# Two adjacent tokens per partition, and weights staged in fp32 and cast on chip: a recurrent attention kernel with a feed-forward layer

## The chip, the cores and the metric

The kernel runs on one core of one Trainium2 chip. The metric is the device time of one execution in microseconds (us), lower is better. Three runs of the kernel before gave a median of 203.13 us (202.38 to 204.61).

The engines are named as in the profile: PE is TensorE's matrix multiply, PEld its weight load, DVE VectorE, ACT ScalarE, POOL GpSimd and SP SyncE. A letter q behind an engine's name is its queue of issued transfers.

## The reference, cut to what matters

```python
# q, k, v, alpha: (batch 4, heads 8, sequence 768, head_dim 48), fp32; alpha between 0.8 and 1.0
for t in range(S):
    state = alpha[:, :, t, :, None] * state + einsum('bhd,bhe->bhde', k[:, :, t], v[:, :, t])
    y[:, :, t] = einsum('bhd,bhde->bhe', q[:, :, t], state)
x = y.transpose(0, 2, 1, 3).reshape(3072, 384)
h = x @ w_in                   # 384 x 2048
out = max(h, 0)**2 @ w_out     # 2048 x 384
```

The state decays by alpha at each token. The kernel treats the sequence in chunks of 128 tokens: with the running sum L of log(alpha) inside a chunk, k is scaled by exp(-L) and q by exp(L), and a masked product of both gives the part of y that comes from inside the chunk. There are 24 chunks: 6 for each of 4 batches.

## The kernel before

A small planner inside the program (the class at the top) takes every operation with an assumed duration and a priority, simulates them, and fixes the order of each engine's instructions and the waits between them. On the chip this order does not change any more.

The parts that the change touches, for one chunk g (cuts marked with "..."):

```python
# one transfer per tensor: 128 tokens on 128 partitions, 8 heads of 48 fp32 (pieces of 192 bytes)
for o, (j, t, nm) in enumerate(((3, alpha, "a"), (0, k, "k"), (1, q, "q"), (2, v, "v"))):
    src = t[b, :, t0:t0 + C, :].rearrange("h p d -> p h d")
    dst = RAW[r][:, j, :].rearrange("p (h d) -> p h d", h=H)
    raw_dma[g, nm] = add("sp", lambda e, ...: e.dma_start(dst, src), 650, p0 - 3 * P + o, ...)

# log(alpha), running sum by a matmul with a triangle of ones, exp(-L) and exp(L)
add("act", lambda e: e.activation(lab, RAW[r][:, 3, :]..., AF.Ln), ...)
def m1(pe):
    ins = pe.matmul(psA[:, 0:HD], LTRI[:], lab)
    ...
add("act", lambda e: e.activation(ASB[a][:, 0, :], psA[:, 0:HD], AF.Exp, scale=-1.0), ...)
add("act", lambda e: e.activation(ASB[a][:, 1, :], psA[:, 0:HD], AF.Exp), ...)

# qks: k and q scaled, in one VectorE instruction; then transposed on TensorE (psT), copied (kqt),
# multiplied (psP), masked (pm), and so on
add("dve", lambda e: e.tensor_tensor(QKS[qs][:, :, :, 0:D], RAW[r][:, 0:2, :]..., ASB[a]..., ALU.mult), ...)
...
# the state update takes the scaled k as it lies, a token per partition
ins = pe.matmul(psY[:, p * 96:p * 96 + 96], QKS[qs][:, 0, 2 * p:2 * p + 2, :]..., VBF[vb][:, p * 96:p * 96 + 96])
...
# weights: GpSimd's software queue casts fp32 to bf16 inside the transfer (page of this kernel: 3.15 MB
# in that queue, which is the weights' size in bf16)
wi_dma[i] = add("pool", w_in_dma(i), 800, -1e6 + 3, writes=[("win", i)], ...)
wo_dma[i] = add("pool", w_out_dma(i), 800, -1e4 + i, writes=[("wout", i)], ...)
```

Of the kernel before, what the change touches and what calls it, by code (L numbers as in the profile page):

```python
# [11 lines left out]
class Op:  # L12
# [3 lines left out]
                 "users", "ndeps", "alts")  # L16

    def __init__(self, eng, fn, cost, prio, name):
        self.eng, self.fn, self.cost, self.prio, self.name = eng, fn, cost, prio, name
        self.deps = {}  # L20
        self.lag = 0
        self.sem = None
        self.users = []
        self.pos = None


class Program:
# [14 lines left out]
    def add(self, eng, fn, cost, prio, reads=(), writes=(), name="", dma=None, lag=0, after=()):  # L42
        op = Op(eng, fn, cost, prio, name)
        op.idx = len(self.ops)
        op.lag = lag
        if dma is not None:
            if dma not in self.dma_sems:
                self.dma_sems[dma] = self.nc.alloc_semaphore("d_" + dma)
                self.dma_count[dma] = 0
            self.dma_count[dma] += 1  # L50
            op.sem = (dma, self.dma_count[dma])
# [28 lines left out]
    def schedule(self):  # L80
# [8 lines left out]
        for op in self.ops:  # L89
            op.ndeps = len(op.deps)  # L90
            for d in op.deps:
                d.users.append(op)
            free[op.eng], avail[op.eng], order[op.eng] = 0.0, [], []
            op.start = 0.0
# [20 lines left out]
        def settle(o, at):  # L115
            nonlocal seq
            for u in o.users:
                u.ndeps -= 1
                u.start = max(u.start, at + (self.HOP + (self.TAIL[o.eng] if o.sem is None else 0) if u.deps[o] else 0))
                if u.ndeps == 0:  # L120
                    heapq.heappush(events, (max(u.start, now), seq, "r", u))
                    seq += 1

        while events:
# [40 lines left out]
            for e in avail:  # L165
                while avail[e] and free[e] <= now + 1e-9:
# [6 lines left out]
                    done += 1  # L173
                    if e == "pe":
# [107 lines left out]
def bass_gla_recurrent__then__act_relu_squared_kernel(  # L282
# [12 lines left out]
    assert H == 8 and D == 48 and DM == HD  # L295
# [6 lines left out]
    G = B * NCH  # L302
    chunks = [(b, c) for c in range(NCH) for b in range(B)]

    NRAW, NLAB, NASB, NQKS, NKQT, NPM, NV, NXB, NRR, NGT, NOSB = 6, 2, 3, 3, 3, 2, 4, 2, 4, 7, 3
# [4 lines left out]
    RAW = sb("raw", [128, 4, HD], FP32, NRAW)  # L310
    LAB = sb("lab", [128, H, DP], BF16, NLAB)
    ASB = sb("asb", [128, 2, HD], BF16, NASB)
    QKS = sb("qks", [128, 2, H, DP], BF16, NQKS)
    KQT = sb("kqt", [128, 2, NPR, 128], BF16, NKQT)
    PM = sb("pm", [128, 2, NPR, 128], BF16, NPM)
    VBF = sb("vbf", [128, HD], BF16, NV)
    SBD = sb("sbd", [128, HD], BF16, B)
    TMP = sb("tmp", [128, HD], FP32, 2)
    ACM = sb("acm", [128, 2 * NPR], FP32, 2)
    XBF = sb("xbf", [128, HD], BF16, NXB)  # L320
    XT = nc.alloc_sbuf_tensor("xt", [128, KT, G * C], BF16)
    LTRI = nc.alloc_sbuf_tensor("ltri", [128, 128], BF16)
    IDENT = nc.alloc_sbuf_tensor("ident", [128, 128], BF16)
    ONES2 = nc.alloc_sbuf_tensor("ones2", [128, 2], BF16)
    HSEL = nc.alloc_sbuf_tensor("hsel", [128, 128], BF16)
    HCOL = nc.alloc_sbuf_tensor("hcol", [128, 2 * NPR], BF16)
# [5 lines left out]
    OSB = sb("osb", [128, DM], FP32, NOSB)  # L332

# [19 lines left out]
    def fill(buf, val):  # L353
        return lambda e: e.memset(buf[:], val)  # L354

    def select(buf, op, fill_v, base, pattern, mult):
        return lambda e: e.affine_select(out=buf[:], in_=buf[:], compare_op=op, fill=fill_v, base=base,
                                         pattern=pattern, channel_multiplier=mult)

    warmed = add("dve", fill(WARM, 0.0), 200, -3e6, writes=[("warm",)], name="warm")  # L360
# [10 lines left out]
    for i, t in enumerate(LAB):  # L371
        add("dve", fill(t, 0.0), 300, -1e6, writes=[("lab", i)])
    for i, t in enumerate(QKS):
        add("dve", fill(t, 0.0), 600, -1e6, writes=[("qks", i)])
    add("pool", fill(LTRI, 1.0), 200, -1e6, writes=[("ltri",)])
    add("pool", select(LTRI, ALU.is_ge, 0.0, 0, [[1, 128]], -1), 300, -1e6, reads=[("ltri",)], writes=[("ltri",)])
    add("pool", fill(ONES2, 1.0), 100, -1e6, writes=[("ones",)])

    for buf, key in ((HSEL, "hsel"), (HCOL, "hcol")):
        add("dve", fill(buf, 0.0), 100, -2e6, writes=[(key,)])  # L380
    for part, key, val in ((HSEL[0:1, 64:128], "hsel", -1000.0), (HSEL[32:33, 0:64], "hsel", -1000.0),
                           (HCOL[0:1, 0:2 * NPR:2], "hcol", 1.0), (HCOL[32:33, 1:2 * NPR:2], "hcol", 1.0)):
        add("dve", lambda e, part=part, val=val: e.memset(part, val), 100, -2e6, reads=[(key,)], writes=[(key,)])

    add("pool", fill(IDENT, 0.0), 200, -1e6 + 1, writes=[("ident",)])
    add("pool", select(IDENT, ALU.not_equal, 1.0, 0, [[-1, 128]], 1), 300, -1e6 + 1, reads=[("ident",)],
        writes=[("ident",)])
    for i in range(B):
        add("pool", fill(SBD[i], 0.0), 400, -1e6 + 2, writes=[("sbd", i)])
# [4 lines left out]
    NWI, NWO = 4, 8  # L394
    FI, FO = FT // NWI, FT // NWO

    def w_in_dma(i):
        src = moe_w_in.rearrange("(kk p) n -> p kk n", p=128)[:, :, i * FI * 128:(i + 1) * FI * 128]
        return lambda e: e.dma_start(WIN[:, :, i * FI * 128:(i + 1) * FI * 128], src)

    def w_out_dma(i):
        src = moe_w_out.rearrange("(kk p) n -> p kk n", p=128)[:, i * FO:(i + 1) * FO, :]
        return lambda e: e.dma_start(WOUT[:, i * FO:(i + 1) * FO, :], src)

    raw_dma = {}
    wi_dma, wo_dma = {}, {}
    LOADS_HELD, W_OUT_FROM = 1, 2

    def held(g):
        return [wi_dma[1]] if g >= LOADS_HELD else []  # L410

    def attention(g):
        b, c = chunks[g]
        t0 = c * C
        p0 = g * P
        r, la, a, qs, kt, pm, vb, xb = (g % n for n in (NRAW, NLAB, NASB, NQKS, NKQT, NPM, NV, NXB))
        first, last = c == 0, c == NCH - 1

        for o, (j, t, nm) in enumerate(((3, alpha, "a"), (0, k, "k"), (1, q, "q"), (2, v, "v"))):
            src = t[b, :, t0:t0 + C, :].rearrange("h p d -> p h d")  # L420
            dst = RAW[r][:, j, :].rearrange("p (h d) -> p h d", h=H)
            raw_dma[g, nm] = add("sp", lambda e, dst=dst, src=src: e.dma_start(dst, src), 650, p0 - 3 * P + o,
                                 writes=[("raw", r, j)], name=f"ld{nm}{g}", dma=f"{nm}{r}", lag=950, after=held(g))

        lab = LAB[la][:, :, 0:D]
        add("act", lambda e: e.activation(lab, RAW[r][:, 3, :].rearrange("p (h d) -> p h d", h=H), AF.Ln),  # L426
            act_ns(HD), p0, reads=[("raw", r, 3)], writes=[("lab", la)], name=f"ln{g}")

        def m1(pe):
            ins = pe.matmul(psA[:, 0:HD], LTRI[:], lab)  # L430
            if not last:
                pe.matmul(psA[:, HD:HD + 2 * NPR], HSEL[:], HCOL[:], start=True, stop=False, skip_group_check=True)
                for p in range(NPR):
                    ins = pe.matmul(psA[:, HD + 2 * p:HD + 2 * p + 2],  # L434
                                    LAB[la][:, 2 * p:2 * p + 2, :].rearrange("p h d -> p (h d)"), ONES2[:],
# [3 lines left out]
        add("pe", m1, pe_ns(HD) + (0 if last else 135), p0 + 300,  # L439
            reads=[("lab", la), ("ltri",), ("ones",), ("hsel",), ("hcol",)], writes=[("ps", "A")], name=f"m1_{g}")  # L440
        add("act", lambda e: e.activation(ASB[a][:, 0, :], psA[:, 0:HD], AF.Exp, scale=-1.0), act_ns(HD), p0 + 500,  # L441
            reads=[("ps", "A")], writes=[("asb", a, 0)], name=f"ei{g}")
        add("act", lambda e: e.activation(ASB[a][:, 1, :], psA[:, 0:HD], AF.Exp), act_ns(HD), p0 + 510,  # L443
            reads=[("ps", "A")], writes=[("asb", a, 1)], name=f"ea{g}")
        if not last:
            add("act", lambda e: e.activation(ACM[g % 2][:, :], psA[:, HD:HD + 2 * NPR], AF.Exp), act_ns(8), p0 + 520,
                reads=[("ps", "A")], writes=[("acm", g % 2)], name=f"ec{g}")

        add("pool", lambda e: e.tensor_copy(VBF[vb][:], RAW[r][:, 2, :]), 500, p0 + 600,  # L449
            reads=[("raw", r, 2)], writes=[("vbf", vb)], name=f"vc{g}")  # L450

        add("dve", lambda e: e.tensor_tensor(QKS[qs][:, :, :, 0:D],  # L452
                                             RAW[r][:, 0:2, :].rearrange("p j (h d) -> p j h d", h=H),
                                             ASB[a][:, :, :].rearrange("p j (h d) -> p j h d", h=H), ALU.mult),
            dve_ns(2 * HD), p0 + 1500, reads=[("raw", r, 0), ("raw", r, 1), ("asb", a, 0), ("asb", a, 1)],
            writes=[("qks", qs)], name=f"qk{g}")

        def tr(pe):
            for j in range(2):
                for p in range(NPR):  # L460
                    o = (j * NPR + p) * 128
                    ins = pe.matmul(psT[:, o:o + 128], QKS[qs][:, j, 2 * p:2 * p + 2, :].rearrange("p h d -> p (h d)"),  # L462
# [173 lines left out]
```

## Time and profile before

| | before |
|---|---|
| median of the first 3 runs | 203.13 us |
| span of the profiled run | 200.4 us |
| first chunk's output leaves PSUM | 44.5 us |
| last chunk's output leaves PSUM | 197.5 us |
| a pair of chunks, in the repeating part | 14.2 us |

The first excerpt is from the profile's page. Its second line gives each engine's busy time and share of the span. The DMA line gives the busy share of the 16 DMA engines, in tenths, in 40 equal slices. The chain line gives the share of the span of each engine in the chain of waits that ended last. In a group line, the numbers behind the bar are busy time, mean ns of one instruction, and idle time before them with its main releaser.

```profile
span 200.4 us, 4825 instructions
...
PE 191.3 (95%) x2013; PEld 136.4 (68%) x2018; DVE 112.1 (56%) x176; ACT 111.0 (55%) x237; POOL 92.8 (46%) x113
...
DMA  6999999999999898999998392451101110110112
...
PE 84%; ACT 5%; DVE 4%; DMA 3%; POOL 2%; issue 1%
...
L452 DVE TENSOR_TENSOR qks<-raw,asb 128x768 bf16<-128x768 f32 x24 | 26.0, 1085 | 16.5 <-ACT asb L443 16.2
```

TensorE is 84% of the chain (6 points of it are dummy matmuls, L363, with which the start is filled). Its busy share of 95% alone would not have shown that: 21.7 us of it are these dummies. The stretch-wise view says more. The columns of the next line are the stretch, its length, and the busy time (with the number of instructions) of PE, PEld, DVE, ACT and POOL, then the granted TensorE clock, the DMA share and GB/s.

```profile
113.55:142.01 28.46, 28.46 (x326) 21.79 (x325) 18.07 (x29) 18.26 (x40) 14.12 (x16) 1.00 0.47 105
```

The stretch was taken from the chain of waits: it lies between the start of two transposes of scaled k and q, four chunks apart.

```profile
113.55 0.51 PE psT L462 x8
114.05 0.65 PE psO L578 x4
114.70 0.66 PE psH L556 x6
...
142.01 0.51 PE psT L462 x8
```

In these 28.46 us TensorE is busy for all 28.46 us, and every link between is a matmul that begins when the one before ends. So a pair of chunks costs 14.2 us of TensorE, and VectorE has 9.0 us of work in it. DMA is busy for eight or nine tenths in nearly every slice until about 110 us. In the first 40 us DMA is busy nearly throughout.

### The profile page before, as it was taken

How to read it: one execution, taken by the hardware profiler on the slowest of the kernel's cores; microseconds unless marked ns; L12 is line 12 of the kernel's file. 1: busy time of each engine (PE TensorE's matmuls, PEld its weight loads, DVE VectorE, ACT ScalarE, POOL GpSimd, SP SyncE). 2: the span in 40 equal slices, each digit the busy share in tenths (PEclk: the TensorE clock that was granted, in tenths of full speed). 3: DMA queues.
4: the chain of work that ended last, by engine and by line, in shares of the span. 5: the costliest groups of instructions: out<-in, count | busy, mean ns of one | idle time of the engine just before them, and what ended most of it. 6: DMA issues, size and time to landing. Idle time of an engine off the chain costs nothing.

```text
span 200.4 us, 4825 instructions
## 1 busy us (share of the span) xinstructions
PE 191.3 (95%) x2013; PEld 136.4 (68%) x2018; DVE 112.1 (56%) x176; ACT 111.0 (55%) x237; POOL 92.8 (46%) x113
## 2 busy tenths in 40 slices
PE   7998798899999999999999999999999999999984
PEld 2456374467777667778778778777787777787752
DVE  5342657575574873665756656845846836562200
ACT  3107354255864845665855747747648557465540
POOL 8306529225546735535626526537346724142430
PEclk9999999999999999999999999999999999999999
DMA  6999999999999898999998392451101110110112
GB/s 126 175 196 180 200 222 163 216 191 215 208 202 219 192 236 170 211 200 221 244 197 210 60 229 68 79 121 41 43 0 42 39 39 3 41 43 0 39 43 79
DMA packets 107094, 27.06 MB, mean 135 GB/s; under 512 B 100416, under 2 KB 107072, under 8 KB 107072
## 3 DMA queue, kind: packets, MB, share of 16 engines
q1 hardware_dynamic: 103296, 23.60, 54.8%
q0 software_dynamic: 3776, 3.15, 10.5%
q8 instruction: 16, 0.26, 0.5%
q14 instruction: 6, 0.05, 0.1%
HBM read 25.17 MB, written 4.72 MB: 149 GB/s over the span
## 4 chain that ended last, share of the span: by engine, by line
PE 84%; ACT 5%; DVE 4%; DMA 3%; POOL 2%; issue 1%
PE psH L556 30%; PE psO L578 30%; PE psO L363 6%; PE psT L462 5%; PE psP L474 3%; DVE qks L452 3%; DMA wout<-in_moe_w_out_dram 3%; PE psY L490 2%; POOL gt L566 2%; PE psT L525 2%; ACT rr L562 2%; PE psA L430 2%; PE psY L487 2%; PE psY L503 1%; ACT asb L443 1%; PE psA L434 1%
## 5 line engine op out<-in xcount | busy, mean ns | idle before, releaser
L566 POOL TENSOR_TENSOR gt<-rr 128x512 bf16<-128x512 bf16 x48 | 51.2, 1066 | 77.9 <-ACT rr L562 75.3
L562 ACT ACTIVATE rr<-psH 128x512 bf16<-128x512 f32 x96 | 57.5, 599 | 43.1 <-PE psH L556 40.1
L578 PE MATMUL psO<-wout,gt 128*128 128x384 bf16 x384 | 76.2, 326 | 0.7 <-ACT osb L585 0.6
L556 PE MATMUL psH<-xt,win 128*128 128x256 bf16 (+1 forms) x624 | 74.6, 265 | 0.3 <-DVE xt L531 0.3
L556 PEld LDWEIGHTS psH<-xt,win 128*128 128x128 bf16 x624 | 54.9, 98 | 11.7 <-DVE xt L531 0.9
L578 PEld LDWEIGHTS psO<-wout,gt 128*128 128x128 bf16 x384 | 34.2, 97 | 17.0 <-ACT osb L585 1.0
L566 DVE TENSOR_TENSOR gt<-rr 128x512 bf16<-128x512 bf16 x48 | 23.2, 484 | 23.3 <-ACT rr L562 23.2
L452 DVE TENSOR_TENSOR qks<-raw,asb 128x768 bf16<-128x768 f32 x24 | 26.0, 1085 | 16.5 <-ACT asb L443 16.2
L479 DVE TENSOR_TENSOR pm<-psP,ltri 128x1024 bf16<-128x1024 f32 x24 | 29.4, 1225 | 7.2 <-PE psP L474 6.9
L449 POOL CAST vbf<-raw 128x384 bf16<-128x384 f32 x24 | 16.1, 674 | 17.1 <-PE psY L503 12.6
L363 PE MATMUL psO<-warm 128*128 128x512 bf16 x73 | 21.7, 422 | 1.4 <-DVE warm L354 1.3
L531 DVE COPY xt<-psT 128x384 bf16<-128x384 bf16 x24 | 8.5, 355 | 25.1 <-PE psT L525 25.1
L441 ACT ACTIVATE asb<-psA 128x384 bf16<-128x384 f32 x24 | 11.7, 488 | 18.6 <-PE psA L434 17.8
L468 DVE COPY kqt<-psT 128x1024 bf16<-128x1024 bf16 x24 | 16.6, 690 | 6.4 <-PE psT L462 5.9
L497 ACT ACTIVATE xbf<-psY 128x384 bf16<-128x384 f32 x24 | 11.8, 493 | 10.7 <-PE psY L490 10.7
L585 ACT ACTIVATE osb<-psO 128x384 f32<-128x384 f32 x24 | 11.8, 491 | 10.1 <-PE psO L578 9.8
L519 POOL TENSOR_TENSOR sbd<-tmp,acm 128x384 bf16<-128x384 f32 x16 | 15.1, 945 | 4.8 <-DVE tmp L517 4.8
L462 PE MATMUL psT<-ident,qks 128*128 128x128 bf16 x192 | 14.8, 220 | 2.1 <-DVE qks L452 1.7
L462 PEld LDWEIGHTS psT<-ident,qks 128*128 128x128 bf16 x192 | 11.7, 98 | 6.0 <-DVE qks L452 2.9
L426 ACT ACTIVATE lab<-raw 128x384 bf16<-128x384 f32 x24 | 12.9, 538 | 2.3 <-DMA raw<-in_alpha_dram 2.3
L363 PEld LDWEIGHTS psO<-warm 128*128 128x128 bf16 x78 | 7.2, 105 | 8.3 <-issue 3.0
L443 ACT ACTIVATE asb<-psA 128x384 bf16<-128x384 f32 x24 | 12.0, 498 | 0.0
(39 smaller groups left out, 122.6 us busy)
## 6 DMA issues: line engine op xcount, KB each, us to landing
raw<-in_alpha_dram SPq DMA_DIRECT2D x24, 192.0 KB, 3.9
raw<-in_k_dram SPq DMA_DIRECT2D x24, 192.0 KB, 3.9
raw<-in_q_dram SPq DMA_DIRECT2D x24, 192.0 KB, 3.7
raw<-in_v_dram SPq DMA_DIRECT2D x24, 192.0 KB, 4.0
out_dram<-osb SPq DMA_DIRECT2D x24, 192.0 KB, 2.7
win<-in_moe_w_in_dram POOLq DMA_DIRECT2D x4, 384.0 KB, 8.3
wout<-in_moe_w_out_dram POOLq DMA_DIRECT2D x8, 192.0 KB, 5.1
```

What stands on the lines that cost most here:

```text
L363: o = Op("pe", lambda pe: pe.matmul(psO[:, 0:512], WARM[:, 0:128], WARM[:], start=not begun, stop=True, skip_group_check=True), 216, 0, "w")
L443: add("act", lambda e: e.activation(ASB[a][:, 1, :], psA[:, 0:HD], AF.Exp), act_ns(HD), p0 + 510, reads=[("ps", "A")], writes=[("asb", a, ...
L449: add("pool", lambda e: e.tensor_copy(VBF[vb][:], RAW[r][:, 2, :]), 500, p0 + 600, reads=[("raw", r, 2)], writes=[("vbf", vb)], name=f"vc{g}")
L452: add("dve", lambda e: e.tensor_tensor(QKS[qs][:, :, :, 0:D], RAW[r][:, 0:2, :].rearrange("p j (h d) -> p j h d", h=H), ASB[a][:, :, :].re ...
L462: ins = pe.matmul(psT[:, o:o + 128], QKS[qs][:, j, 2 * p:2 * p + 2, :].rearrange("p h d -> p (h d)"), IDENT[:], is_transpose=True)
L468: add("dve", lambda e: e.tensor_copy(KQT[kt][:].rearrange("p j n s -> p (j n s)"), psT[:, :]), dve_ns(1024, 2), p0 + 3000, reads=[("ps", " ...
L479: add("dve", lambda e: e.tensor_tensor(PM[pm][:].rearrange("p j n s -> p (j n) s"), psP[:, :, :].rearrange("p j (n s) -> p (j n) s", n=NPR ...
L519: add("pool", lambda e: e.tensor_tensor(sb3, TMP[g % 2][:].rearrange("p (n d) -> p n d", d=D), acm, ALU.mult), 800, p0 + 8000, reads=[("tm ...
L556: ins = pe.matmul(psH[hb][:, i * n:(i + 1) * n], WIN[:, kk, fj * 128:(fj + 1) * 128], XT[:, kk, g0 * C:g0 * C + n], start=(kk == 0), stop= ...
L562: add("act", lambda e, hb=hb, rb=rb: e.activation(RR[rb][:], psH[hb][:], AF.Relu), act_ns(512), pu + 600, reads=[("ps", "H", hb)], writes= ...
L566: add(eng, lambda e, rb=rb, dst=dst: e.tensor_tensor(dst, RR[rb][:].rearrange("p (i s) -> p i s", i=per), RR[rb][:].rearrange("p (i s) -> ...
L578: ins = pe.matmul(psO[:, 0:DM], GT[gt][:, fj, ti * C:(ti + 1) * C], WOUT[:, fj, :], start=(fj == 0), stop=(fj == FT - 1))
```

## The change

The intent: alpha, k and q are read with two adjacent tokens on one partition, which makes pieces of 384 bytes out of 192. Two batches then fill the 128 partitions, 64 each, and make a *unit* of two chunks. One running sum now serves a unit: it is the sum of log(alpha of the even token times alpha of the odd one), so the odd token's own alpha has to be taken into account apart: k of the even token is multiplied by alpha of the odd token, and q of the even token is divided by it. The state update still needs the scaled k with a token per partition, which four small transfers inside the chip restore ("the shuffle", tile ks). The weights are read by the hardware queues in fp32 into a staging buffer and cast by VectorE, ScalarE and GpSimd. The loads of a unit are placed in the queue behind the shuffle of the unit before.

```diff
+    units = [(b, c) for c in range(NCH) for b in range(0, B, 2)]
+    def attention(u):
+        gate = shuffles.get(u - 1, [])
+        al = RAW[r][:, 2, :, :]
+        for o, (j, t, nm) in enumerate(((2, alpha, "a"), (0, k, "k"), (1, q, "q"))):
+            for ab in range(2):
+                src = t[b0 + ab, :, t0:t0 + C, :].rearrange("h (p j) d -> p h (j d)", j=2)
+                dst = RAW[r][ab * HP:(ab + 1) * HP, j, :, :]
+                add("sp", lambda e, dst=dst, src=src: e.dma_start(dst, src), 350, ..., behind=gate)
 ...
+        add("dve", lambda e: e.tensor_tensor(a01, al[:, :, 0:D], al[:, :, D:2 * D], ALU.mult), dve_ns(HD), pu - 500, ...)
+        add("act", lambda e: e.activation(lab, a01, AF.Ln), act_ns(HD), pu, ...)
+        add("dve", lambda e: e.tensor_tensor(k0, k0, al[:, :, D:2 * D], ALU.mult), dve_ns(HD), pu, ...)
+        add("dve", lambda e: e.reciprocal(RAL[0][:]..., al[:, :, D:2 * D]), dve_ns(HD), pu - 200, ...)
+        add("pool", lambda e: e.tensor_tensor(q0, q0, RAL[0][:]..., ALU.mult), 900, pu - 200, ...)
 ...                                    # one running sum, one pair of exponentials a unit; qks as two instructions
+            for ab in range(2):
+                for j in range(2):     # the shuffle
+                    mv = add("sp", lambda e, dst=dst, src=src: e.dma_start(dst, src), 300, pu - 5 * P,
+                        reads=[("qks", qs, 0)], writes=[("ks", ks, ab, j)], ...)
+                    shuffles.setdefault(u, []).append(mv)
 ...
-                wi_dma[i] = add("pool", w_in_dma(i), 800, ...)
+        add("sp", w_in_load(i), 250, prio, writes=[("stg", i)], ...)
+        for kk, eng in enumerate(("dve", "act", "pool")):
+            add(eng, cast(eng, WIN[:, kk, ...], STG[i][...]), COPY_NS[eng](n), ...)
 ...                                    # the same for w_out, in halves and quarters of a piece
```

The cuts leave out the constants, buffer counts, the mask for the new token order, and the planner's new argument `behind`, which orders two operations in the plan without a wait on the chip. The assumed durations are 350 ns for the issue of a load, 300 for one of the shuffle, and 480 ns for `dve_ns(HD)`.

## The prediction

> **What bounds the kernel now.** From about 68 us on, the chain of waits is matmuls back to back. In it the same transposes come at 113.55 and 142.01 us, four chunks apart: 7.1 us of TensorE per chunk, 171 us for 24. The span is 200.4 us, the last eviction and store take about 3 us, so some 27 us are lost, nearly all before 68 us. There the timeline shows 21.7 us of dummy warm-up matmuls, the first feed-forward matmul at 14.6 us, and the chain's longest wait, 5.2 us for w_out (31.9 to 37.1 us). The queue table puts 131 us of busy DMA into the span, and the slices are 90% or more until 110 us. DMA bounds the start, TensorE the rest; VectorE is 65% busy there.
>
> **DMA.** Before: 98,304 pieces of 192 bytes and 3,072 stores of 1,536 bytes. The last windows put a store piece at about 71 ns, which leaves 15.7 ns for 192 bytes. A line through both gives (estimate) 23.5 ns for 384 bytes, so alpha, k and q at 260 GB/s instead of 196. A unit (two chunks) then costs 6.5 us instead of 8.0. The weights, 21 us now, should cost about 18 us. [...] All of w_out lands at about 35 us instead of 37.
>
> **Removed.** Half of the cumulative-sum matmuls: about 0.3 us per chunk becomes 0.15, so 3.6 us of TensorE. ScalarE: 1.7 us per unit (logs and exponentials halved). GpSimd: 9.2 us of DMA issues.
>
> **Added.** Casts: about 6 us each on VectorE and GpSimd, 4.4 on ScalarE, in the first 40 us. Per unit on VectorE, two products of 384 columns (0.55 us each, as the 128x384 sums) and a reciprocal; on GpSimd a product (0.95 us). Loads of a unit wait behind the previous unit's k shuffle; latency plus load plus chain is about 11 us, within the 14 us period.
>
> **The reciprocal is the doubt.** [...] I give the slow one 45%.
>
> **Sum.** Fast reciprocal: 167 us of TensorE, 22 lost at the start, 3 at the end, 2.7 between span and timed run: 195 us. Slow: [...] start and end as before: 205 to 210 us. Weighted: 197 us, eight in ten between 188 and 210. Chances: faster 0.52, same 0.28, slower 0.20.
>
> **What would show it.** Mean duration of the reciprocal[...]; VectorE's busy share in 80 to 160 us (85% or 95+%); whether TensorE is still busy throughout there and the chain still matmuls; DMA time per 384-byte piece (23.5 ns); landing of w_out (35 us); first feed-forward matmul (16 us).
>
> **What would make it wrong.** A slow reciprocal hidden in VectorE slack; half-partition transfers that are much slower; a static order stalling TensorE on VectorE; loads gated on the shuffle starving units 2 and 3.

The text on record is cut where no trace of this case shows what it rested on: how much slower transfers into 64 partitions might be, and how long a slow reciprocal might take. Terms of its sum are thereby missing. In full it weighed two cases. With a reciprocal as quick as the 128x384 sums, which took 0.55 us in the kernel before, it came to 195 us. With a slow one it came to 205 to 210 us. Weighed, at 45% for the slow one, the forecast was 197 us.

## The result, and the profile after

A ratio in this document is the mean time of one kernel's fast runs over that of the other's fast runs of the same rounds, so it is not quite the ratio of the medians that are quoted.

| | before | after |
|---|---|---|
| median of 4 runs each, same rounds | 202.75 us | 236.35 us (233.82 to 237.45; one of the four slow) |
| ratio | 1 | 1.160 (95% interval 1.147 to 1.172) |
| first / last chunk's output leaves PSUM | 44.5 / 197.5 us | 43.1 / 230.7 us |
| a unit (two chunks), repeating part | 14.2 us | about 17.1 us (16.6 to 18.7 between 90 and 177 us) |
| busy share of the 16 DMA engines x span | 131 us | 140 us |

The kernel is 16% slower, far outside the predicted range. The first chunk ends 1.4 us earlier than before, but that is no measure of the start. By 80 us the kernel before had begun 96 of the 384 matmuls of the second feed-forward layer, and this one 64. At the 180 that the kernel before began in the next 80 us, these 32 are an estimated 14 us, in part because the first units run at the slower rate too. That rate is the rest: a unit takes 17.1 - 14.2 = 2.9 us more. For all 12 units that would be 35 us, and the medians differ by 33.6; but this sum counts the start as if it were repeating part, so that it fits proves little. The experiments below separate the two: some 23 us go when the repeating part is mended, and some 9 to 10 us stay in the start.

The page after, same views as before:

```profile
span 234.4 us, 4753 instructions
...
PE 193.5 (83%) x1882; PEld 133.0 (57%) x1885; DVE 168.8 (72%) x223; ACT 100.7 (43%) x199; POOL 111.5 (48%) x124
...
DMA  5999999819358239329339269359859202011112
...
PE 30%; DVE 27%; SPq 13%; DMA 13%; issue 10%; ACT 4%; POOL 1%; DVEq 0%
...
L515 DVE TENSOR_TENSOR qks<-raw,asb 128x768 bf16<-128x768 f32 x24 | 35.2, 1494 | 1.9 <-POOL raw L486 0.9
...
L484 DVE RECIPROCAL ral<-raw 128x384 f32<-128x384 f32 x12 | 30.5, 2544 | 0.0
```

No engine is at its limit: DVE has 72%, and the chain is shared among TensorE, VectorE, the issuing of transfers (SPq) and the transfers. That is the picture of a loop of latencies, not of a full engine. The DMA line shows it too: where it stood at nine tenths until 110 us, it now swings between one and nine, a burst for each unit. The reciprocal takes 2,544 ns for 384 elements per partition, where the planner assumed 480.

The repeating part as a stretch, with the same columns as before; one unit, from one product of the alphas to the next:

```profile
90.05:107.53 17.48, 13.87 (x147) 9.80 (x145) 13.67 (x17) 7.97 (x16) 8.31 (x9) 1.00 0.59 132
```

TensorE is busy for 13.87 of 17.48 us and VectorE for 13.67; both wait. The granted clock is 1.00 here, so the lower clock that this run shows in some slices before 83 us and in one near 190 us (its mean is 0.96) does not set the rate.

The chain of waits of one unit (start, duration, and what):

```profile
100.78 0.48 SPq L541
...
103.22 0.64 SPq L462
...
103.91 3.60 DMA raw<-in_alpha_dram
...
107.53 0.56 DVE a L476
108.09 0.29 DVE ral L484
108.38 2.09 issue
110.47 0.49 DVE raw L482
110.97 1.14 DVE pm L561
...
112.15 0.34 PE psY L569 x4
...
115.04 0.60 ACT rr L652
115.64 0.39 ACT asb L504
...
116.05 1.85 DVE qks L515
...
117.91 0.48 SPq L541
```

This is a loop: it begins and ends with the issue of a shuffle (L541), 17.13 us apart. Reading down: four shuffle issues of about 0.6 us each (2.44), the first issue of an alpha load (0.69), the load (3.62), the product of the alphas (0.56), the reciprocal (2.38 until the next instruction starts; the chain names 2.09 of it "issue", but VectorE is in the reciprocal all that time, as its own stream shows), the k product (0.50), a mask product of the unit before (1.18), matmuls of the unit before and of the feed-forward layer (2.89), a relu and the exponential (1.01), and the scaling of k (1.86), which allows the next shuffle. They add up to 17.13.

Four of these ten terms do not belong to the path from load to shuffle by their data: the reciprocal, the mask product, the matmuls and the relu of 0.60 us. They stand in it because an engine has placed them there in its order. Together they are 7.05 us; the rest, 10.1 us, is close to the 11 us that the prediction gave the loop. The log (0.52 us) and the running sum (0.33 us) do belong to the path by their data, but they lie hidden beside these four. The log ended at 108.6 us; the running sum's matmul, which waits for nothing else, began at 115.0, behind the matmuls that stand before it in TensorE's order.

VectorE's own stream shows something else: in this unit it waits only 0.43 us for the load (in brackets), so it would be little faster without the loop. The experiments come back to that.

```profile
107.53 0.56 DVE L476 TENSOR_TENSOR a<-raw 128x384 f32<-128x384 f32 x1 [0.43 <-DMA raw<-in_alpha_dram]
```

### The profile page after: what moved, and what is told of

Its sections match the earlier page's. It is cut to its first block, busy times and chain, and to the rows that moved or that the text cites. A ratio compares the mean times of both kernels' runs of the same rounds, so it can differ in the third digit from the quotient of the medians.

```text
span 234.4 us, 4753 instructions
## 1 busy us (share of the span) xinstructions
PE 193.5 (83%) x1882; PEld 133.0 (57%) x1885; DVE 168.8 (72%) x223; ACT 100.7 (43%) x199; POOL 111.5 (48%) x124
## 3 DMA queue, kind: packets, MB, share of 16 engines
q1 hardware_dynamic: 74112, 32.52, 59.8%
## 4 chain that ended last, share of the span: by engine, by line
PE 30%; DVE 27%; SPq 13%; DMA 13%; issue 10%; ACT 4%; POOL 1%; DVEq 0%
DMA raw<-in_alpha_dram 13%; PE psH L645 12%; PE psO L669 9%; DVE qks L515 9%; SPq L541 7%; DVE pm L561 5%; SPq L462 4%; DVE a L476 3%; DVE ral L484 3%; DVE gt L656 3%; DVE raw L482 2%; ACT rr L652 2%; SPq L468 2%; PE psT L526 2%; PE psY L569 1%
## 5 line engine op out<-in xcount | busy, mean ns | idle before, releaser
L645 PE MATMUL psH<-xt,win 128*128 128x256 bf16 x576 | 77.2, 276 | 0.4 <-ACT rr L652 0.3
L561 DVE TENSOR_TENSOR pm<-psP,mask 128x1024 bf16<-128x1024 f32 x24 | 29.2, 1218 | 14.2 <-PE psP L555 14.1
L515 DVE TENSOR_TENSOR qks<-raw,asb 128x768 bf16<-128x768 f32 x24 | 35.2, 1494 | 1.9 <-POOL raw L486 0.9
L486 POOL TENSOR_TENSOR raw<-raw,ral 128x384 f32<-128x384 f32 x12 | 13.6, 1134 | 36.7 <-DMA raw<-in_q_dram 17.7
L484 DVE RECIPROCAL ral<-raw 128x384 f32<-128x384 f32 x12 | 30.5, 2544 | 0.0
L620 POOL TENSOR_TENSOR sbd<-tmp,acm 128x384 bf16<-128x384 f32 x16 | 19.8, 1241 | 1.5 <-DVE tmp L618 1.5
L569 PE MATMUL psY<-sbd,kqt 128*128 128x96 bf16 x80 | 7.1, 214 | 12.9 <-DVE pm L561 12.9
L511 POOL CAST vbf<-rav 128x384 bf16<-128x384 f32 x24 | 15.1, 638 | 2.7 <-DMA rav<-in_v_dram 2.5
L569 PEld LDWEIGHTS psY<-sbd,kqt 128*128 128x128 bf16 x80 | 5.1, 101 | 16.5 <-DVE pm L561 15.2
L618 DVE TENSOR_TENSOR tmp<-psY,sbd 128x384 f32<-128x384 f32 x16 | 8.8, 550 | 7.4 <-PE psY L602 7.4
```

The source lines that it names most:

```text
L484: add("dve", lambda e: e.reciprocal(RAL[0][:].rearrange("p (h d) -> p h d", h=H), al[:, :, D:2 * D]), dve_ns(HD), pu - 200, reads=raw(2), ...
L515: add("dve", lambda e, t=t: e.tensor_tensor(QKS[qs][:, t, :, :, 0:D].rearrange("p j h d -> p h j d"), RAW[r][:, t, :, :].rearrange("p h (j ...
L561: add("dve", lambda e, pm=pm: e.tensor_tensor(PM[pm][:].rearrange("p j n s -> p (j n) s"), psP[:, :, :].rearrange("p j (n s) -> p (j n) s" ...
L620: add("pool", lambda e, sb3=sb3, acm=acm, ab=ab: e.tensor_tensor(sb3, TMP[ab][:].rearrange("p (n d) -> p n d", d=D), acm, ALU.mult), 800, ...
L645: ins = pe.matmul(psH[hb][:, i * n:(i + 1) * n], WIN[:, kk, fj * 128:(fj + 1) * 128], XT[:, kk, g0 * C:g0 * C + n], start=(kk == 0), stop= ...
```

## The experiments

All kernels differ from the kernel after by the edit shown, unless it says otherwise. Each was run with 3 timed rounds beside the kernel before, on one chip per group; the medians of before in the four groups lie between 202.4 and 202.8 us. Every edit but the cheap product makes the planner order the engines anew. Three theories stood at the outset. In one, a loop through shuffle, loads and VectorE sets the rate, because the loads are gated (the loop). In the second, the reciprocal fills VectorE, or upsets a plan that was made for a cheap one (capacity, plan; "VECTORE" and "PLAN" in the expectations). In the third, loads into 64 partitions are too slow ("LOADS"). From e5 on, "STREAM" is the theory that VectorE's instructions, in their order and with their waits for other engines, set the rate.

### First group: take out the reciprocal, the gate, both, or the planner's errors

**e1_cheap_recip.** The reciprocal is replaced by a product of 0.55 us in the same place; the plan is unchanged. The result is wrong (relative error 0.33).

```diff
-        add("dve", lambda e: e.reciprocal(RAL[0][:]..., al[:, :, D:2 * D]), dve_ns(HD),
+        add("dve", lambda e: e.tensor_tensor(RAL[0][:]..., al[:, :, D:2 * D], al[:, :, D:2 * D], ALU.mult), dve_ns(HD),
```

> The reciprocal becomes a product of the same shape (planned cost unchanged, so every engine has the same order; the result is wrong on purpose). LOOP theory (the changed kernel is paced by a loop of 17.1 us per unit: shuffle issue, alpha load, product, reciprocal, product, scale, next shuffle): the loop loses 2.54 - 0.55 = 2.0 us, 11 times, so 236 becomes about 214 us (210 to 219). VECTORE theory (VectorE has too much work, the loop is only a symptom): VectorE falls from 13 to 11 us per unit and TensorE is the bound again, 195 to 205 us. LOADS theory (half-partition loads are too slow): no change, 230 us or more.

Measured: 222.0 us (221.31 to 223.4), ratio to before 1.098 (1.092 to 1.104). That is some 14 us off for 12 x 2.0 us of removed work: less than the loop theory gave (210 to 219 us), very far from a VectorE that was merely full, and too fast for loads that set the rate (230 us or more). The chain of waits shows what stood ready behind the reciprocal:

```profile
95.87 3.61 DMA raw<-in_k_dram
...
99.51 1.29 DVE raw L482
```

The k load is issued two transfers after alpha's. Its landing now ends the wait before the k product, and a unit takes 16.1 us instead of 17.1.

**e2_no_gate.** The loads are no longer held behind the shuffle.

```diff
-        gate = shuffles.get(u - 1, [])
+        gate = []
```

> Only the rule is taken away that a unit's loads are issued after the previous unit's k shuffle (the static order of all engines is planned anew). LOOP theory: no loop is left, TensorE (14 us per unit) or VectorE (13 us) paces: 198 to 210 us. VECTORE theory: the reciprocals are all still there, 225 us or more. LOADS theory: no change, 230 us or more.

Measured: 251.66 us (249.58 to 253.66; three fast runs), ratio 1.240 (1.231 to 1.249). It is slower than the kernel after. The loop theory missed; the number lies in the open range of the other two (225 and 230 us or more), but for a reason that none of them gave. Without the gate the planner takes preparations of later units forward, and the single buffer of the reciprocal closes another loop:

```profile
115.14 4.18 DMA raw<-in_q_dram
...
119.39 1.01 POOL raw L486
...
120.43 2.55 DVE ral L484
...
135.52 4.13 DMA raw<-in_q_dram
...
139.71 1.00 POOL raw L486
...
140.74 2.55 DVE ral L484
```

A reciprocal waits until GpSimd has used the last one, which waits for a q load. As VectorE works in order, everything behind that reciprocal waits too. The new loop is 20.4 us long (135.52 - 115.14). So this edit did not show what the gate costs: it removed one loop and made a longer one.

**e3_both.** Both edits above; wrong result.

```diff
-        gate = shuffles.get(u - 1, [])
+        gate = []
-        ... e.reciprocal(RAL[0][:]..., al[:, :, D:2 * D]) ...
+        ... e.tensor_tensor(RAL[0][:]..., al[:, :, D:2 * D], al[:, :, D:2 * D], ALU.mult) ...
```

> Gate taken away and cheap product in place of the reciprocal (wrong result on purpose). LOOP theory: as without the gate, at most 8 us less: 193 to 205 us. VECTORE theory: clearly below the run without the gate, by 20 us or more. LOADS theory: 225 us or more.

Measured: 242.85 us (242.6 to 243.94), ratio 1.201 (1.194 to 1.209). The cheap product takes 9 us off here, and the result stays worse than the kernel after, for the reason just given.

**e4_true_plan.** The planner is told the measured durations; the gate and the work stay.

```diff
-  load issue 350, reciprocal dve_ns(HD) [480], shuffle issue 300, store issue 200
+  load issue 660, reciprocal 2460,             shuffle issue 600, store issue 620
```

> The planner is told the measured costs: 2460 ns for the reciprocal (480 before), 600 to 660 ns for each transfer issue (200 to 350 before); operations and gate unchanged. LOOP theory: the loop has the same members, so 225 to 238 us. PLAN theory (the static order is bad because it was planned with wrong costs): 205 to 216 us.

Measured: 229.33 us (227.27 to 230.03), ratio 1.132 (1.124 to 1.139). A true plan is worth about 7 us, as the loop theory expected (225 to 238 us). In its chain the mask product is now ahead of the reciprocal, but the alpha load is still in it for 3.48 us behind four shuffle issues. So the plan's errors were a part of the loss and not its main cause.

### Second group: the gate a unit earlier, and the two halves of the change apart

**e5_gate_two_back.** The loads are held behind the shuffle of the unit before the last one, so that they can be a unit ahead.

```diff
-        gate = shuffles.get(u - 1, [])
+        gate = shuffles.get(u - 2, [])
```

> A unit's loads are issued after the shuffle of the unit two before, not one before; VectorE keeps its repeating order, only the loads come one unit earlier. (The run without any gate was slower because the plan then ran units ahead; this one does not let it.) LOOP theory (the load behind the shuffle is what paces): the shuffle issues and the alpha load, some 6.6 us, leave the loop; TensorE paces, 203 to 216 us. STREAM theory (VectorE's own in-order stream, 14 us of work and 3 us of round trips to TensorE, is the pace; in the trace it waits only 0.43 us for alpha in a 17.1 us unit): 0.4 us x 11 less, 228 to 234 us.

Measured: 236.51 us (235.23 to 238.42), ratio 1.166 (1.159 to 1.174). No change, and outside both ranges, but the test was not clean. In the new plan the product of the alphas, the reciprocal and the k product had moved a unit ahead together with the loads, so they waited for them as before, and the period stayed at 17.1 us.

**e6_gate_two_back_cheap.** e5 and the cheap product; wrong result.

```diff
-        gate = shuffles.get(u - 1, [])
+        gate = shuffles.get(u - 2, [])
-        ... e.reciprocal(RAL[0][:]..., al[:, :, D:2 * D]) ...
+        ... e.tensor_tensor(RAL[0][:]..., al[:, :, D:2 * D], al[:, :, D:2 * D], ALU.mult) ...
```

> As the run before, with the cheap product in place of the reciprocal and the same order as it (wrong result on purpose). STREAM theory: the stream loses 2.0 us per unit and no load holds it, 14.7 us per unit: 206 to 213 us, that is 10 to 15 us below the cheap product with the old gate (222). LOOP theory: at most 4 us below the run before this one.

Measured: 230.82 us (229.38 to 232.22), ratio 1.135 (1.127 to 1.143). A miss: the chain still runs from the shuffle over a load to the products, 16.1 us per unit.

**e7_weights_only.** The kernel before, with only the weights changed: fp32 staging by SyncE's queue, and the casts.

```diff
-    wi_dma[i] = add("pool", w_in_dma(i), 800, ...)          # before.py, casts inside the transfer
+    wi_dma[i] = add("sp", w_in_load(i), 250, ...); casts on dve, act, pool
+    if g == 2 + i:                                          # piece i of w_out
+        w_out_piece(i, -1e4 + i, [raw_dma[g - 1, "a"]])
```

> The kernel before with only the weights part of the change: four fp32 pieces of each weight by the hardware queue and casts on three engines. If the weights part has a share in the loss: 206 us or more. My theory: it is neutral or a little better than the kernel before, 197 to 204 us, with all of w_out landed a few us earlier.

Measured: 207.61 us (206.27 to 210.14; one run, the profiled one, was in the slow state), ratio 1.021 (1.014 to 1.027), which the 2% rule calls unclear. It missed my range; taken alone it gave the weights a share in the loss. But the last cast of w_out began at 56.6 us (in the profiled, slow run), so the placing of the pieces, one for each chunk, was mine to doubt. The fourth group tests that.

**e8_tokens_only.** The kernel after, with the weights again by GpSimd's software queue and cast inside the transfer.

```diff
-                w_in_piece(i, (2 * W_IN_AT[i] - 4) * P + i)
+                add("pool", w_in_dma(i), 800, -1e6 + 3, writes=[("win", i)], ...)
-                w_out_piece(i, (2 * W_OUT_AT[i] - 4) * P + i)
+                add("pool", w_out_dma(i), 800, -1e4 + i, writes=[("wout", i)], ...)
```

> The changed kernel with its weights loaded as before (software queue, cast in the transfer). My theory: the loss is in the token part, 230 to 240 us, as the whole change. If the weights part had a share: 225 us or less.

Measured: 242.46 us (241.74 to 243.68), ratio 1.195 (1.190 to 1.201), a little above the expected range. The whole loss lies in the tokens' part; the weights' part rather helps beside it.

### Third group: loads truly a unit ahead, with and without the reciprocal

**e9_early_loads_held.** As e5, but the three preparations on VectorE are ordered behind the last copy of the unit before, so their place nearly stays and only the loads are early. (One mask product and one square, pm and gt, now come behind the preparations instead of before them.)

```diff
+    evicts = {}                                  # the last kqt copy of each unit
-        gate = shuffles.get(u - 1, [])
+        gate = shuffles.get(u - 2, [])
+        held = [evicts[u - 1]] if u else []
-   product of alphas, k product, reciprocal:  name=...)
+   product of alphas, k product, reciprocal:  name=..., behind=held)
```

> Loads behind the shuffle of two units before, as in the earlier try, but this time the preparation (alpha product, reciprocal, k product) is held in the plan behind the previous unit's last transpose eviction, so that VectorE really keeps its order and only the loads come a unit earlier (in the earlier try the preparation moved ahead with them and the loop was the same). STREAM theory (VectorE in order, 14 us of work and 3 us of round trips, ties with the load loop at 17 us): 226 to 234 us, and no wait for alpha or k is left in the repeating part. LOOP theory: 205 to 216 us.

Measured: 231.01 us (229.54 to 232.08), ratio 1.139 (1.132 to 1.146). This is in the range of the stream theory. The load loop is gone, but the time hardly falls: this refutes the loop as the sole cause. The period is 17.3 us, no shorter than in the kernel after; the 5 us were gained earlier, as the sixth unit's product of the alphas begins at 81.6 us instead of 90.0. Here is VectorE in one unit, in order of time (start, duration, what, and in brackets the idle time before it and what ended it):

```profile
98.97 0.55 DVE L478 TENSOR_TENSOR a<-raw 128x384 f32<-128x384 f32 x1
99.43 2.54 DVE L486 RECIPROCAL ral<-raw 128x384 f32<-128x384 f32 x1
101.90 0.49 DVE L484 TENSOR_TENSOR raw<-raw 128x384 f32<-128x384 f32 x1
102.31 1.21 DVE L563 TENSOR_TENSOR pm<-psP,mask 128x1024 bf16<-128x1024 f32 x1
...
105.14 1.22 DVE L563 TENSOR_TENSOR pm<-psP,mask 128x1024 bf16<-128x1024 f32 x1 [0.63 <-PE psP L557]
...
107.34 0.43 DVE L658 TENSOR_TENSOR gt<-rr 128x512 bf16<-128x512 bf16 x1 [0.71 <-ACT rr L654]
108.57 0.56 DVE L620 TENSOR_TENSOR tmp<-psY,sbd 128x384 f32<-128x384 f32 x1 [0.80 <-PE psY L604]
...
110.40 3.34 DVE L517 TENSOR_TENSOR qks<-raw,asb 128x768 bf16<-128x768 f32 x2 [0.20 <-ACT asb L506]
...
115.70 0.69 DVE L535 COPY kqt<-psT 128x1024 bf16<-128x1024 bf16 x1 [0.71 <-PE psT L528]
116.31 0.55 DVE L478 TENSOR_TENSOR a<-raw 128x384 f32<-128x384 f32 x1
```

No line waits for a load any more. VectorE works for 14.3 us of the 17.34, and the five idle times in brackets, 3.05 us, are round trips: it hands work to TensorE or ScalarE and its next instruction in order needs the answer. The same stretch by engine:

```profile
98.97:116.31 17.34, 14.44 (x159) 10.31 (x157) 14.29 (x19) 7.88 (x16) 9.54 (x9) 1.00 0.61 130
```

So there was a second chain of nearly the same length: VectorE's in-order stream with its round trips. It is bound at 82% busy, and a count of its work alone (14.3 us against 14.2 of TensorE) would call the two even.

**e10_early_loads_cheap.** e9 and the cheap product; wrong result.

```diff
   e9, and
-        ... e.reciprocal(RAL[0][:]..., al[:, :, D:2 * D]) ...
+        ... e.tensor_tensor(RAL[0][:]..., al[:, :, D:2 * D], al[:, :, D:2 * D], ALU.mult) ...
```

> As the run before, with a cheap product in place of the reciprocal, planned cost and so order unchanged (wrong result on purpose). STREAM theory, both of the tied chains shortened: about 14.6 us per unit, 204 to 214 us, at least 8 us below the cheap product with the old gate (222). If a third thing paces: 218 us or more.

Measured: 216.96 us (216.4 to 217.62), ratio 1.070 (1.065 to 1.075). The range was just missed, the period is 15.6 us. The early loads alone took 5 us off, the cheap product alone 14, both 19 us. Between e9 and e10 the plan is the same, so these 14 us come from the reciprocal's duration alone. What is left in its chain of waits is 4.59 us in a row on VectorE, behind which the next transposes stand:

```profile
104.28 0.39 ACT asb L506
...
104.70 3.34 DVE qks L517 x2
108.04 0.64 DVE gt L658
108.68 0.61 DVE kqt L535
...
109.34 0.62 PE psT L528 x8
```

The two scaling instructions take 3.34 us together. Each scales as many elements as the one of the kernel before, whose mean was 1.09 us; the fastest in the trace of after took 0.95. The slow ones lie beside GpSimd instructions: in after, the pair that begins at 98.91 us took 1.84 and 1.58 us, and GpSimd has products running from 97.93 to 101.44. The kernel before, with its old layout, shows the like: the five scalings that no GpSimd instruction overlaps took 0.96 us each, and one beside two of them 1.74 (19.47 us). But another took 0.95 us (56.82 us) with a GpSimd cast running beside it all the time, so overlap alone does not decide it. What slows the scalings was not tested by a run of its own.

**e11_recip_on_act.** e9, with 1/alpha on ScalarE as exp(-log(alpha)); the result is correct.

```diff
   e9, and
-        add("dve", lambda e: e.reciprocal(RAL[0][:]..., al[:, :, D:2 * D]), dve_ns(HD), ...
+        add("act", lambda e: e.activation(ral, al[:, :, D:2 * D], AF.Ln), 520, pu - 200, ..., behind=held)
+        add("act", lambda e: e.activation(ral, ral, AF.Exp, scale=-1.0), 500, pu - 199, ...)
```

> Early loads and held order as above, and 1/alpha computed on ScalarE as exp(-ln alpha), 1.0 us per unit there instead of 2.54 us on VectorE; the result is right. 204 to 215 us, within 4 us of the cheap product. A candidate for the best version of the token layout; I do not expect it under the kernel before (202.7).

Measured: 213.23 us (210.06 to 215.05; two of four runs slow), ratio 1.043 (1.032 to 1.054), inside the expected range. The two ScalarE instructions took 0.52 and 0.51 us (21.62 and 22.64 us in its trace), the expected 1.0 us together. Two units as stretches:

```profile
93.58:107.66 14.08, 14.08 (x159) 10.56 (x157) 11.91 (x18) 8.81 (x18) 10.75 (x11) 1.00 0.76 172
107.66:122.16 14.50, 14.29 (x159) 10.50 (x157) 12.05 (x17) 8.81 (x18) 10.27 (x11) 1.00 0.73 155
```

TensorE is full again, and a unit costs 14.3 us as a pair of chunks did before. With both chains shortened, the repeating loss is gone; so loads into 64 partitions do not set the rate. (The plan is new here, so e11 and e10 are not a clean pair: the scalings, too, became faster, 1.23 us in the mean instead of 1.50.) No gain over before is left in it either: the predicted 0.3 us of TensorE that a unit should save does not show.

The remaining 4% lies in the start. Without the dummy matmuls, TensorE had begun 691 of its 1,940 matmuls by 80 us before, and 551 of 1,830 in e11 (counts of the trace, in which some records can be missing). Of the 384 of the second feed-forward layer it was 96 before and 80 in e11; these 16 are an estimated 7 us, counted as above, of the 7.8 by which the profiled spans differ. The last w_out piece in e11 lands at 48.2 us, against 40.6 before. The granted clock is not the reason: it was 0.96 in e11's first 80 us and 1.00 in e10's, and e10 had begun the same 80 by then.

**e12_recip_on_act_plan.** e11, with the measured durations in the planner.

```diff
   e11, and
-  load issue 350, shuffle issue 300, store issue 200, alpha and k product dve_ns(HD), qks dve_ns(2 * HD), POOL 900 and 800
+  load issue 660, shuffle issue 600, store issue 620, alpha and k product 560, qks 1300, POOL 1100
```

> As the run before, with the planner told measured costs for issues, the new products and the scaling. 0 to 8 us below the run before (the same correction gave 7 us on the changed kernel): 198 to 212 us.

Measured: 212.82 us (211.35 to 213.15), ratio 1.047 (1.040 to 1.054). No gain, and just outside the range. Its first chunk ends at 41.7 us, before that of the kernel before, and still it had begun only 522 matmuls by 80 us: an early first output is no measure of a good start.

### Fourth group: the weights' part again, and the best tokens with it

**e13_weights_act_queue.** e7 with the weights issued from ScalarE's hardware queue. In this kernel and in e15 below the planner adds a wait of a load for the readers of the staging buffer; a form without it had a race.

```diff
   e7, and
-        add("sp", w_in_load(i), 250, ...)    and the same for w_out
+        add("act", w_in_load(i), 550, ...)   and the same for w_out
```

> Weights part alone on the kernel before, the pieces issued from ScalarE's hardware queue beside the loads instead of between them (w_out piece i still waits for the alpha of chunk 1+i). If the placement lost the 2%: 198 to 204 us. If the staging and casts lost it: 206 us or more.

Measured: 203.87 us (203.39 to 204.19), ratio 1.005 (0.9995 to 1.010).

**e14_weights_w_out_first.** e7 with w_out right behind w_in, as the staging buffers come free.

```diff
   e7, and
-            if g == 2 + i:
-                w_out_piece(i, -1e4 + i, [raw_dma[g - 1, "a"]])
+            if g == 2:
+                w_out_piece(i, -1e5 + i, [])
```

> Weights part alone, all on the loads' queue, w_out pieces as early as their staging buffers come free. w_out cast by 30 to 35 us instead of 56. If the placement lost the 2%: 199 to 205 us. If the staging and casts lost it: 206 us or more.

Measured: 203.52 us (202.46 to 204.09), ratio 1.004 (0.998 to 1.010). Both say the same: the weights' part alone is neutral, and the 2% of e7 came from the placing.

**e15_best_tokens_act_queue.** e11 with the weights on ScalarE's queue, to mend the start.

```diff
   e11, and
-        add("sp", w_in_load(i), 250, ...)    and the same for w_out
+        add("act", w_in_load(i), 550, ...)   and the same for w_out
```

> Best version of the token layout (early loads, 1/alpha on ScalarE) with the weights on ScalarE's hardware queue. Its repeating part is already paced by TensorE (14.4 us per unit against 14.2 before), so a gain can come only from the start, where its first chunk ends at 50 us against 44.5 before: 203 to 211 us. Under 199 would beat the kernel before.

Measured: 217.87 us (216.81 to 218.95), ratio 1.074 (1.067 to 1.081): a miss, it is worse than e11. The last w_out load now lands at 30.8 us, but on a second queue the weights get ahead of the tokens: the log of the first alphas, which waits for their load, begins at 12.5 us instead of 5.6.

```profile
12.51 0.53 ACT L481 ACTIVATE lab<-a 128x384 bf16<-128x384 f32 x1
```

In e11 the same line of the view in order of time reads:

```profile
5.64 0.52 ACT L481 ACTIVATE lab<-a 128x384 bf16<-128x384 f32 x1
```

By 80 us e15 had begun 505 matmuls, fewer than e11. No kernel beats the kernel before. Which order of tokens and weights would give the new layout a start as good as before's stays open.

## Why the prediction was wrong

**What bounds the kernel before: right.** TensorE has 14.2 us of work in a pair of chunks and is busy in all of them; e11, which shortens both new chains, comes back to 14.3.

**The step that failed: "Loads of a unit wait behind the previous unit's k shuffle; latency plus load plus chain is about 11 us, within the 14 us period."** The loop measured 17.13 us. The 11 us were nearly right for what depends on the loads by its data (10.1 us, without the hidden log and running sum). What was left out is the work of others that stands between in the engines' order: reciprocal 2.38, mask product 1.18, matmuls 2.89 and relu 0.60, together 7.05 us. As the loads cannot start before the loop has come round, it is paid in every unit, 2.9 us more than the 14.2 that TensorE needs. It is not the whole loss: the repeating part accounts for some 23 of the 34 us (e11), and the other 9 to 10 lie in the start, where the prediction allowed "22 lost at the start", some 5 less than the 27 before.

**The second failure: VectorE judged by its sum of work.** The slow case was a sum of VectorE's work, with start and end as before: 205 to 210 us. The measured work, 14.3 us a unit in e9, gives much the same: 12 x 14.3 = 172, and with the prediction's 27 us of start, 3 of end and 2.7 between span and timed run an estimated 204 us. But e9 took 231 us. VectorE, which works in its fixed order and hands over to other engines, did not get to 100%: with 3.05 us of round trips its stream took 17.3 us. The predicted sign, VectorE at 95% or more in 80 to 160 us, was also not there: it was 78% busy in that stretch.

**Two chains of equal length.** The load loop (17.1) and VectorE's stream (17.3) were nearly tied, which is why early loads, which mend the loop alone, moved little: 5 us. The reciprocal was in both chains, so a cheap one alone took 14 us; both edits took 19, and early loads with the reciprocal off VectorE 23. Not run: the reciprocal on ScalarE with the old gate. How much of e11's gain came from its new order is therefore not separated.

**The reciprocal: the doubt was right, the total drawn from it was not.** The quick case had 0.55 us; measured were 2.54, or 6.6 ns per element (2,544 / 384). That is about five times a product of the same size (0.49 to 0.56 us for most products in the repeating part). The duration that the slow case assumed was shown by no trace and is cut. The 45% that this case got was fair; the 205 to 210 us that it was given were the miss.

**DMA: the pieces about right, the sum wrong.** The median time of a 384-byte piece was 22 ns and the mean 27.3, against a predicted 23.5. (The 1,536-byte store pieces of before, one end of the prediction's line, took 65 ns in its trace, where the prediction read 71.) But, summed over the trace's records of transfers and divided by 16 engines, alpha, k and q fell only from 72 to 63 us, v rose from 24 to 28, and the shuffle added 10.5; the weights took 18.3 instead of 21 (predicted 18). The total rose from 131 us (65.3% of 200.4) to 140 us (59.8% of 234.4). The prediction's fear that transfers into 64 partitions are much slower does not show in the median piece. A test of like with like is v: its pieces kept their 192 bytes and now go into 64 partitions instead of 128, and their median stayed at 15 ns (mean 15.6 before, 18.3 after). Neither set the rate: after 40 us, DMA was some 60% busy (0.57 to 0.63 in the stretches of after).

**TensorE and the rest.** The 3.6 us of removed running sums stayed invisible, since TensorE was not the bound; in e11, where it was, they did not show either. The first feed-forward matmul came at 19.6 us (predicted 16, before 14.6). All of w_out had landed at 38.6 us (predicted 35), and its casts began between 31.6 and 41.4 us. All casts together took 4.1 us on VectorE, 6.3 on GpSimd and 4.6 on ScalarE (predicted 6, 6 and 4.4), and GpSimd's product 1.13 us in the mean (predicted 0.95). Before, the last of w_out's eight pieces landed at 40.6 us; the 37 of the prediction was a wait for an earlier piece. The slower scaling, 1.49 us a piece instead of 1.09, whose cause no run shows, was not in the sum at all. Of the four warnings at the prediction's end, two named the real causes: a static order that stalls TensorE on VectorE, and loads gated on the shuffle. The second was feared for units 2 and 3 only; it was so in every unit.

**The weights: right.** Neutral alone (e13, e14).

What stays open: the start of the new layout, some 9 to 10 us in e11 and e12 (by the ratios of fast runs), of which the traces show late weights (e11) or late tokens (e15), but no run that has both early.

## What to carry to other kernels

Where a transfer is queued behind a result, follow the loop from that result to the next one over every instruction that the engines have between, not only over those that depend on it: here 10 us by data were 17 by order. An engine that works in a fixed order and needs answers from others can bind well below 100% busy (VectorE did at 82%); add its round trips before comparing it with the bound. And when a removed cost brings little, look for a second chain of the same length and take both away in one run before calling the cost harmless.
